# Reordering the parts of a time unit in a chunked recurrence on one Trainium2 core: output products to the unit's end, transposes moved together

## The chip, the core and the metric

One NeuronCore of a Trainium2 chip runs the whole program. The metric is device time in microseconds; lower is better. Engine names as in the profile: PE (TensorE) matmuls, PEld its weight loads, DVE (VectorE), ACT (ScalarE), POOL (GpSimd), SP (SyncE, which issues the DMAs here).

## What is computed

A linear recurrence over 768 tokens for 4 x 8 heads with a 40 x 40 state, then two feed-forward layers. Cut to what matters:

```python
for t in range(S):                                   # S = 768
    y[:, :, t] = np.einsum('bhd,bhde->bhe', rt, state)
    Sa = np.einsum('bhde,bhe->bhd', state, at)
    state_decay = state * wt[:, :, None, :] - np.einsum('bhd,bhe->bhde', Sa, bt)
    state = state_decay + np.einsum('bhd,bhe->bhde', vt, kt)
...
x = relu(x @ w_in); x = (x * sigmoid(conv3(x))) @ w_out          # layer 1
h = relu(x @ w_in2); out = (u * (w_spatial @ norm(v) + b)) @ w_out2   # layer 2
```

The change touches the recurrence alone.

## The kernel before

The tokens are cut into 6 groups of 128 (two chunks of 64 each) and the batch into 4, which gives 24 units kk = 0 .. 23 of 8 heads each (`units`, line 390). Two units of one token group with neighbouring batches make a pair, which shares its loads and its tiles. Four generators hold a unit's work, and each `yield` in them ends a part:

- `A` (lines 148 to 183), 5 parts, prepares a unit 9 units ahead (LA=9): 8 transposes of AR and their two scaled copies (tile bdA, L157, L159); then for each half of the heads four transposes of P and a copy to PT by ACT (L167, L168), two parts; then for each half four products of PT with bdA, masked by DVE into G (L174, L175), two parts. After the last one of a pair, four stores of G's triangles to DRAM are due 3 parts later (L181, TBL=3).
- `Bp` (231 to 297), 4 parts from token group 1 on, for the unit kk+1: pf and its copies (L272, L275, L278), px and its copies into bdN (L284, L287), then two parts of pw (L295) with their scaled copies WT by ACT (L296).
- `Cp` (317 to 343), 4 parts, carries the state: pu (L327) and its copies to Z by ACT (L329), pm (L338) and two DVE steps to the next VM (L340, L342), once per chunk.
- `Dp` (344 to 388), 6 parts, makes the output of the unit kk-1: z0, z1 (transposes pz and pv, L360, L366, and ACT's copies), S0, S1 (products pS, L373, masked by DVE into SS, L374), y0, y1 (16 pairs of small products each into one PSUM tile py, L381, L383); after y1 DVE multiplies py into lnA (L385), and for a pair's second unit a store of x is due 2 parts later (L387).

`run`'s main loop (line 478) is a hand-written order: the string ORDER has 19 letters, and part z takes the next part of the generator that the letter names. After each part `tick` issues what has come due, `pump` runs 1.25 steps on average of a background list (a triangular solve, `subst`, L206 and L208 on DVE, which is present in some units and absent in others), and the table SCHED, chosen by the parity of kk, starts the loads of the pair 5 pairs on. In even units these are il, araw, lnA, the product G (POOL), `dup`, P (l_P, L115) and `ar`; in odd units the one entry is "pm": `l_pm` (L145), the product of the whole P tile with the decays il, on DVE (PMV=1).

Since LA=9, A in an odd unit prepares the first unit of a pair, whose P has just been multiplied in that same unit; A in an even unit prepares the pair's second unit. A runs in the units 0 to 14 (unit 0 prepares two). Units 15 to 23 have no A; there the preparation of the next layer's weights (`later_layer`) fills DVE and ACT.

In this part of the program every engine runs in the order in which the code issues; all tiles named "ps" share 6 PSUM buffers, P has 6 buffers, ZV, bdR, SS and PT two, bdA, bdN and il one. Unit 9 is the stretch from 262.59 to 278.19 us of the trace, unit 11 begins at 293.89; both are odd, 9 with the background solve and 11 without it until late.

Of the kernel before, what the change touches and what calls it, by code (L numbers as in the profile page):

```python
# [11 lines left out]
def attention(tc, keep, ident, vr,bk,w,a, x, spare=None):  # L12
# [4 lines left out]
    with ExitStack() as ctx:  # L17
# [71 lines left out]
        def tick():  # L89
            now[0]+=1  # L90
            for d in [d for d in due if d[0]<=now[0]]:
                due.remove(d); d[1]()
# [300 lines left out]
        def pump(m):  # L393
            while m>0 and (bg or bg2):
                q=bg or bg2
                try: next(q[0])
                except StopIteration: q.pop(0); continue
                m-=1
# [10 lines left out]
        with tc.manual_schedule(engines={mybir.EngineType.SP,mybir.EngineType.DVE,mybir.EngineType.Activation}):  # L409
# [58 lines left out]
            with tc.manual_schedule():  # L468
# [9 lines left out]
                for kk in range(NK):  # L478
# [6 lines left out]
                    z=-1  # L485
                    for g in ORDER if kk<TAIL else ORDER2:
                        if g=='W':
# [7 lines left out]
                        tick(); acc+=RATE0 if kk<3 else RATE if kk<14 else RATE2; pump(int(acc)); acc-=int(acc)  # L495
                        for s,f in SCHED[(kk+LA+1)%2]+SCHEDC[kk%2]:
                            if s==z:
# [13 lines left out]
PUA=1  # L511
WM=2
ORDER2="DCCDDBCBACDADDABBAA"
ORDER="CDCBDDCBDDACABBDAAA"
LA=9
L4T=14
RATE=1.25
RATE2=1.25
RATE0=1.4
SCHED=[[[1, "il"], [11, "araw"], [12, "ln"], [14, "g"], [15, "dup"], [16, "P"], [17, "ar"]], [[5, "pm"]]]  # L520
SCHEDC=[[[6, "Z"]], [[10, "V"]]]
SUB=5
TBL=3
# [543 lines left out]
```

## Time and profile before

| | |
|---|---|
| timed runs, median (lowest to highest) | 960.11 us (960.07 to 965.37) |
| the profiled execution's own time | 955.54 us |
| its span, first to last instruction | 953.8 us |
| mean granted TensorE clock | 0.948 |
| busy in the span: PE / PEld / DVE / ACT / POOL | 91% / 83% / 69% / 56% / 21% |

The profiled execution is one run of its own, 4.6 us below the median of the timed ones. The units of the recurrence lie between 100 and 483 us; before them are loads and the first units' preparation, behind them the two layers. A busy share is an average over these stages.

### The profile page before, as it was taken

Reading aid. Unit: us, or ns where it says so; the run is one execution under the profiler, and the core shown is the slowest. Engines: PE = TensorE matmul, PEld = TensorE weight load, DVE = VectorE, ACT = ScalarE, POOL = GpSimd, SP = SyncE. Lnnn points to the kernel's source line nnn. Section 1 sums busy time; section 2 is a strip of 40 time slices with the busy share of each in tenths; the row PEclk is TensorE's granted clock in tenths of the full one; section 3 lists DMA queues with packets and bytes.
Section 4 is the critical chain, followed back from the end, with each engine's and each line's share of the span. In section 5 each row is a group of like instructions: output and inputs, shape, how many; then the busy total and the mean of one; then the engine's idle time right before and its main releaser. Section 6 shows DMA issues by size and latency. Waiting matters only on the chain. (4 is left out here: it accounts for less than half of the span.)

```text
span 953.8 us, 23470 instructions
## 1 busy us (share of the span) xinstructions
PE 863.3 (91%) x9575; PEld 793.1 (83%) x9575; DVE 661.8 (69%) x1503; ACT 535.7 (56%) x1166; POOL 204.9 (21%) x268
## 2 busy tenths in 40 slices
PE   0877699999999998989897799999999899998997
PEld 0566588999999998878786689998999889998997
DVE  6886785596794968976769976388725877368841
ACT  0444567778677776578655663366515654266521
POOL 2100110112111212123310002144223431234221
PEclk9975589999999998899989999999999999999999
DMA  8988594646557546235411320111001100011001
GB/s 215 211 187 225 121 212 101 153 91 152 110 124 178 95 99 156 65 103 131 125 63 58 107 80 19 42 48 36 23 25 42 56 1 26 21 53 32 1 1 45
DMA packets 149189, 86.70 MB, mean 91 GB/s; under 512 B 124176, under 2 KB 138256, under 8 KB 147152
## 3 DMA queue, kind: packets, MB, share of 16 engines
q1 hardware_dynamic: 148800, 84.78, 36.3%
q8 instruction: 77, 1.26, 0.6%
q14 instruction: 40, 0.33, 0.1%
q10 hardware_dynamic: 272, 0.33, 0.1%
HBM read 61.24 MB, written 23.86 MB: 89 GB/s over the span
## 5 line engine op out<-in xcount | busy, mean ns | idle before, releaser
L690 PE MATMUL psp<-spt,vv 128*128 128x384 f32 x576 | 105.6, 338 | 0.5 <-DVE vv L818 0.3
L690 PE MATMUL ph<-XT,G 128*128 128x386 f32 x512 | 101.9, 344 | 0.8 <-DVE XT L723 0.8
L690 PEld LDWEIGHTS psp<-spt,vv 128*128 128x128 f32 x576 | 100.2, 188 | 2.2 <-ACT vv L815 1.1
L690 PEld LDWEIGHTS ph<-XT,G 128*128 128x128 f32 x512 | 93.1, 192 | 1.3 <-DVE XT L723 1.0
L766 PE MATMUL acc<-gh,G 128*128 128x384 f32 x320 | 70.9, 347 | 17.1 <-ACT gh L750 9.3
L752 POOL TENSOR_TENSOR gl<-c,gh 128x384 fp32r<-128x384 f32 x48 | 66.3, 1381 | 90.0 <-ACT gh L750 78.1
L331 POOL COPY ZU<-ZU 64x320 f32<-64x320 f32 x48 | 25.7, 535 | 245.6 <-ACT ZU L329 245.6
L766 PEld LDWEIGHTS acc<-gh,G 128*128 128x128 f32 x320 | 55.6, 189 | 25.7 <-ACT gh L750 13.4
L835 DVE TENSOR_TENSOR psp<-psp,bb 128x384 f32<-128x384 f32 x32 | 18.1, 566 | 70.6 <-PE psp L690 70.5
L206 DVE TENSOR_TENSOR tmp<-L 128x30 f32<-128x30 f32 (+9 forms) x150 | 58.4, 389 | 8.6 <-DMA L<-tb 4.7
L748 DVE TENSOR_TENSOR c<-h,c 128x384 f32<-128x384 f32 x64 | 39.3, 614 | 33.2 <-ACT c L745 33.0
L750 ACT CAST gh<-c 128x384 fp32r<-128x384 f32 x64 | 32.9, 514 | 52.4 <-DVE c L748 51.0
L174 PE MATMUL p<-PT,bdA 80*128 80x128 f32 x384 | 57.3, 306 | 4.6 <-ACT PT L168 4.2
L174 PEld LDWEIGHTS p<-PT,bdA 80*128 80x128 f32 x384 | 52.6, 215 | 8.8 <-ACT PT L168 8.6
L373 PE MATMUL pS<-bdR,ZV 80*128 80x128 f32 x384 | 56.3, 291 | 2.8 <-ACT ZV L367 2.8
L839 ACT CAST zh<-u 128x384 fp32r<-128x384 f32 x28 | 14.4, 513 | 73.2 <-DVE u L836 73.2
L208 DVE TENSOR_TENSOR L<-L,tmp 128x30 f32<-128x30 f32 (+9 forms) x150 | 52.4, 349 | 3.8
L381 PE MATMUL py<-P,SS 128*64 128x40 f32 x768 | 52.2, 240 | 2.8 <-DVE SS L374 2.5
L295 PE MATMUL pw<-bdN,G 128*104 128x128 f32 x384 | 52.4, 295 | 1.0 <-issue 0.9
L373 PEld LDWEIGHTS pS<-bdR,ZV 80*128 80x128 f32 x384 | 48.5, 198 | 4.6 <-ACT ZV L367 3.3
L383 PE MATMUL py<-ZV,bdR 80*64 80x40 f32 x768 | 51.1, 237 | 0.0
L840 POOL TENSOR_TENSOR zl<-u,zh 128x384 fp32r<-128x384 f32 x28 | 28.6, 1020 | 101.0 <-ACT zh L839 91.5
(185 smaller groups left out, 2093.3 us busy)
## 6 DMA issues: line engine op xcount, KB each, us to landing
P<-in_bk_dram SPq DMA_DIRECT2D x12, 640.0 KB, 5.8
ZU<-in_vr_dram SPq DMA_DIRECT2D x12, 640.0 KB, 7.0
lq<-in_w_dram SPq DMA_DIRECT2D x12, 320.0 KB, 6.9
araw<-in_a_dram SPq DMA_DIRECT2D x12, 320.0 KB, 6.8
lam<-lq SPq DMA_DIRECT2D x12, 320.0 KB, 5.0
lnA<-lam SPq DMA_DIRECT2D x12, 320.0 KB, 7.7
ilam<-lq SPq DMA_DIRECT2D x12, 320.0 KB, 5.6
il<-ilam SPq DMA_DIRECT2D x24, 160.0 KB, 4.3
```

Of the source, the lines that this page charges most:

```text
L174: T.matmul(p3[:,j],lhsT=bdA[:,g*4+j].rearrange("p c t -> p (c t)"),rhs=PTs[g][:,j],start=True,stop=True)
L206: V.tensor_tensor(t,L[:,j+1:HB,j:j+1].to_broadcast([128,m,j]),L[:,j:j+1,0:j].to_broadcast([128,m,j]),ALU.mult)
L208: V.tensor_tensor(L[:,j+1:HB,0:j],L[:,j+1:HB,0:j],t,ALU.add)
L295: T.matmul(p[:104,j],lhsT=G[:,h0+g*4+j,C:],rhs=N[:,g*4+j],start=True,stop=True)
L373: T.matmul(p[:,j].rearrange("p c t -> p (c t)"),lhsT=ZV[:,j,0:2*C],rhs=bdR[:,j].rearrange("p c t -> p (c t)"),start=True,stop=True)
L381: T.matmul(py[c*C:(c+1)*C,h],lhsT=SS[:,j,c],rhs=P[:,h0+h,c],start=True,stop=False)
L383: T.matmul(py[c*C:(c+1)*C,h],lhsT=bdR[:,j,c],rhs=ZV[:,j,2*C:],start=False,stop=True)
L690: L.tc.nc.tensor.matmul(out,lhsT=l,rhs=r,start=start and i==0,stop=stop and i==len(prs)-1)
L748: V.tensor_tensor(c,h[:,1:TH+1],c,ALU.mult)
L750: AC.copy(gh,c)
L752: def low(v): v.tensor_tensor(gl,c,gh.bitcast(F32),ALU.subtract)
L766: nc.tensor.matmul(acc[m],lhsT=l,rhs=r,start=f==0 and z<5 and z in (0,1,3),stop=f==NF-1 and z>=5)
```

## The change

Three settings change; no operation is added or taken away. With the 19 parts numbered 0 to 18:

- D's last two parts, y0 and y1, go from the places 9 and 15 to 17 and 18, the end of the unit. A goes from 10, 12, 16, 17, 18 to 9, 11, 12, 15, 16, so that its two P transposes stand together ahead of the two pw parts (13, 14 as before). C's last part (pm of the second chunk) goes from 11 to 10.
- P's load (even units) goes from 16 to 18, since the buffer that it takes is released by y1 of the same unit.
- P's product with the decays (odd units) goes from 5 to 8.

```diff
-ORDER="CDCBDDCBDDACABBDAAA"
+ORDER="CDCBDDCBDACAABBAADD"
...
-SCHED=[[[1, "il"], [11, "araw"], [12, "ln"], [14, "g"], [15, "dup"], [16, "P"], [17, "ar"]], [[5, "pm"]]]
+SCHED=[[[1, "il"], [11, "araw"], [12, "ln"], [14, "g"], [15, "dup"], [18, "P"], [17, "ar"]], [[8, "pm"]]]
```

On PE, in an A-carrying unit (unit 10), from px to the products of PT (rows of the first py part are left out; pS, p_.. with AR, pm and p_.. with P are the parts S1, bdA, pm and the transposes of P):

```order
-L157 MATMUL p_4026<-ident,AR 80x64 x8
-L338 MATMUL pm<-ZU,P 40x40 x8
-L167 MATMUL p_4053<-ident,P 80x128 x4
+L284 MATMUL px<-F,D_3541 32x32 x16
+L373 MATMUL pS<-bdR,ZV 128x128 x4
+L157 MATMUL p_4009<-ident,AR 80x64 x8
+L338 MATMUL pm<-ZU,P 40x40 x8
+L167 MATMUL p_4034<-ident,P 80x128 x4
+L167 MATMUL p_4043<-ident,P 80x128 x4
 L295 MATMUL pw<-bdN,G 104x128 x8
```

The transposes of AR now follow S1 directly, and the second group of P transposes stands ahead of pw instead of behind y1; the sixteen py rows that stood around these now stand behind the last PT product, directly ahead of the next unit's pu.

On DVE, in unit 9 (SS are the masked pS parts, L206 and L208 the background solve, P the product with the decays, m and VM the two steps behind pm):

```order
 L374 TENSOR_TENSOR SS<-pS,mS 128x512
 L206 TENSOR_TENSOR tmp<-L 128x228
-L145 TENSOR_TENSOR P<-P,il 128x1280
 L208 TENSOR_TENSOR L<-L,tmp 128x12x19
...
 L374 TENSOR_TENSOR SS<-pS,mS 128x512
 L206 TENSOR_TENSOR tmp<-L 128x210
+L145 TENSOR_TENSOR P<-P,il 128x1280
 L208 TENSOR_TENSOR L<-L,tmp 128x10x21
+L340 TENSOR_TENSOR m<-pm,VM 40x320
+L342 TENSOR_TENSOR VM<-m,lamC 40x8x40
```

The product of P stood between the first and the second masked pS and now stands behind the second.

On SP, at the end of an even unit (D is a load for the solve's results, tb the stores of G's triangles, x the store of the output):

```order
-L229 DMA D_4071<-dd_129 32x16x32 x2
-L387 DMA x<-lnA 128x2x320
-L115 DMA P<-in_bk_dram 128x1280
+L229 DMA D_4061<-dd_129 32x16x32 x2
 L181 DMA tb_124<-G 32x16x32 x4
+L115 DMA P<-in_bk_dram 128x1280
+L387 DMA x<-lnA 128x2x320
```

P's load was issued ahead of the four triangle stores and is now issued behind them, and x's store goes from ahead of P's load to behind it.

## Rows read from the trace of the kernel before

**Rows 1.** Busy time by stage; columns: window, length, then PE, PEld, DVE, ACT, POOL, clock, DMA

```profile
190.00:340.00 150.00, 149.17 (x2634) 136.86 (x2634) 116.51 (x270) 111.04 (x238) 26.09 (x42) 1.00 0.58 123
356.00:483.00 127.00, 115.50 (x2109) 105.81 (x2106) 93.92 (x192) 84.65 (x212) 36.37 (x63) 0.92 0.45 118
```

**Rows 2.** PE in order of time, unit 9; columns: start, length, work

```profile
270.00 0.32 PE L381 MATMUL py<-P,SS 128*64 128x40 f32 x4
...
271.06 0.64 PE L157 MATMUL p<-ident,AR 64*80 64x64 f32 x8
271.63 0.81 PE L338 MATMUL pm<-ZU,P 128*40 128x40 f32 x16
272.37 0.64 PE L167 MATMUL p<-ident,P 128*80 128x128 f32 x4
272.84 1.91 PE L295 MATMUL pw<-bdN,G 128*104 128x128 f32 x16
274.68 0.32 PE L381 MATMUL py<-P,SS 128*64 128x40 f32 x4
...
275.74 0.64 PE L167 MATMUL p<-ident,P 128*80 128x128 f32 x4
```

**Rows 3.** DVE in order of time, unit 9

```profile
269.04 0.69 DVE L374 TENSOR_TENSOR SS<-pS,mS 128x512 f32<-128x512 f32 x1
...
269.95 1.49 DVE L145 TENSOR_TENSOR P<-P,il 128x1280 f32<-128x1280 f32 x1
271.35 0.39 DVE L208 TENSOR_TENSOR L<-L,tmp 128x228 f32<-128x228 f32 x1
...
272.50 0.68 DVE L374 TENSOR_TENSOR SS<-pS,mS 128x512 f32<-128x512 f32 x1
```

**Rows 4.** DVE in order of time, unit 11, with the idle time before and its releaser

```profile
301.02 0.69 DVE L374 TENSOR_TENSOR SS<-pS,mS 128x512 f32<-128x512 f32 x1 [0.22 <-PE pS L373]
```

**Rows 5.** PE in order of time, the last product of unit 8 and unit 9's start

```profile
260.39 2.27 PE L174 MATMUL p<-PT,bdA 80*128 80x128 f32 x16
262.59 0.67 PE L327 MATMUL pu<-VM,WT 104*64 104x40 f32 x16
```

**Rows 6.** PE in order of time, unit 0 and units 15 and 16

```profile
126.39 2.05 PE L174 MATMUL p<-PT,bdA 80*128 80x128 f32 x16 [0.88 <-ACT PT L168]
...
364.03 0.32 PE L381 MATMUL py<-P,SS 128*64 128x40 f32 x4 [1.00 <-DVE SS L374]
...
364.99 0.78 PE L338 MATMUL pm<-ZU,P 128*40 128x40 f32 x16
...
375.36 0.67 PE L327 MATMUL pu<-VM,WT 104*64 104x40 f32 x16 [1.18 <-DVE VM L342]
...
378.67 0.44 PE L381 MATMUL py<-P,SS 128*64 128x40 f32 x4
...
380.40 1.27 PE L338 MATMUL pm<-ZU,P 128*40 128x40 f32 x16
```

**Rows 7.** All waits, 100 to 484 us: engine, line, releaser, total, times, longest

```profile
PEld pm L338 <- ACT ZU L329: 5.0, 16, 1.3
```

**Rows 8.** DMA issues on SP at unit 10's end, and P's load issue to landing

```profile
292.58 0.44 SPq L387 DMA_DIRECT2D x<-lnA  x1
293.11 0.42 SPq L115 DMA_DIRECT2D P<-in_bk_dram  x1
294.72 2.07 SPq L181 DMA_DIRECT2D tb<-G  x4
...
DMA to landing us min/median/max: 4.2/5.8/8.8
```

**Rows 9.** Busy time in three short stretches, columns as in rows 1

```profile
372.90:376.40 3.50, 2.32 (x57) 2.11 (x56) 3.25 (x10) 2.04 (x7) 0.18 (x1) 1.00 0.68 134
...
376.40:383.20 6.80, 6.80 (x79) 6.43 (x73) 5.76 (x15) 0.98 (x3) 0.45 (x1) 0.50 0.40 61
...
403.70:407.10 3.40, 2.15 (x36) 1.92 (x30) 3.13 (x10) 2.43 (x7) 0.42 (x2) 1.00 0.11 23
```

## The prediction, made before the changed kernel was run

> **What bounds the kernel now.** I read the busy time by stage first. From 190 to 340 us, the heart of the recurrence, PE is busy 149.2 of 150.0 us with the clock at its full level [rows 1]: there nothing can be won by filling gaps, only by making the parts themselves shorter, and every wait that the change puts before PE is paid in full. From 356 to 483 us PE has 11.5 us of idle time and a mean clock of 0.92 [rows 1]; there fillers can pay. Behind 483 us the change does nothing. Next I read PE in order of time through one odd unit [rows 2] and DVE beside it [rows 3], since an odd unit is where P's product with the decays moves, then DVE in an odd unit without the background solve [rows 4].
>
> **Parts that come closer together on PE.** A y part takes 0.96 us where the next part has small products too (364.03 to 364.99, [rows 6]), but 1.06 us where transposes follow it (270.00 to 271.06, and 274.68 to 275.74, [rows 2]): a change of the kind of product costs about 0.10 us. In a unit with A the order was S1, y0, bdA, pm, P transposes, pw, y1, P transposes, G products, pu; it becomes S1, bdA, pm, P transposes, pw, G products, y0, y1, pu. The joints y0-bdA, pw-y1 and y1-P transposes go, three of 0.10 us, in 14 units (1 to 14): -4.2 us. No row shows the joint S1-bdA or P transposes-P transposes apart; bounds for the whole term are 0 and 6.
>
> **G products that waited for PT.** In unit 8 the two G parts take 2.20 us (260.39 to 262.59, [rows 5]), while sixteen instructions of the same 128-column shape, pw, take 1.84 us (272.84 to 274.68, [rows 2]). The second G part waits for ACT's copy of the second PT, which was issued just ahead. With pw between the transposes and the G parts that copy is long done: 0.36 us in the six even units 2 to 12, -2.2 us. Unit 0 has one such wait on its own, 0.88 us [rows 6]: -0.9 us.
>
> **The units without A.** y0 in unit 15 waits 1.00 us for the masked SS; put behind pm and pw it would not. pu in unit 16 waits 1.18 us for VM [rows 6], which DVE reaches late; DVE's multiply behind y1 now comes after more of its background work, so some of this goes as well. But DVE is the late engine there, busy 93.9 of 127 us in bursts, and a PE that arrives sooner waits again for it: between 0 and -2.2 us, I take -1.5 us. The price on the other side: pm of the second chunk loses the cover of y0 (0.96 to 1.06 us) against ACT's copy of Z. Such waits are there already, 16 of 5.0 us in all [rows 7]; each could grow by up to 1 us, or not at all. I take +1.0 us.
>
> **P's product, the term that decides.** The first P transposes of an odd unit cannot start before the product is done (1.49 us on DVE, [rows 3]). Before, it stood behind the first SS, at 269.95 us in unit 9, and its reader came at 272.37 us: a spare 0.9 us after the product's end. Now it stands behind the second SS. With PE going on at 270.00 us, where y0 stood, bdA takes 0.57 us and pm 0.74 us [rows 2], so PE wants P at 271.31 us. DVE, if as late as now, starts the second SS at 272.50 - 1.40 = 271.10 us (the product no longer ahead of it), then 0.69 for the mask, 0.39 for one solve step and 1.49 for the product [rows 3]: 273.67 us, so PE waits 2.4 us. If DVE were not late, SS would start with PE's 270.00 and a tenth, and the wait would be 1.4 us. I take 1.9 us for the three odd units in the middle of a solve (5, 9, 13). Without the solve (3, 7, 11) DVE starts the second SS as soon as S1 ends, at 301.02 us [rows 4], and needs 0.69 + 1.49 = 2.18 us, while PE needs 0.57 + 0.74 = 1.31 us: 0.9 us each. Unit 1 is between 0 and 2.4 us; I take 1.0. Sum: 5.7 + 2.7 + 1.0 = +9.4 us. Behind the waiting transposes on PE stand the second group, pw, G, both y and the next unit's pu, all of which shift; behind them on DVE stand m and VM, which nobody wants before the next token group; ACT's PT and WT copies wait with PE.
>
> **P's load and the queues.** It waits for y1 of the even unit to free its buffer, so it moves from 293.11 us, 0.8 us ahead of the unit's end (unit 11 begins at 293.89), to just behind it, and on SP now stands behind four triangle stores that take 2.07 us to issue [rows 8]; their G is ready two y parts ahead of the unit's end, so I put the load's issue at 0.9 to 1.3 us into the odd unit. With the median of 5.8 us to landing [rows 8] it is there at about 7 us; the product's place on DVE is 7.8 us (301.71 - 293.89) without the solve, later with it. So the load costs nothing, with a cover of under 1 us. What is pushed back on SP is x's store, which nobody reads before the layers. ZV, bdR and SS are overwritten one unit on, behind y1 on PE's own queue: no cost. py now holds its PSUM buffer for two parts instead of seven; no row shows a wait for one, so I count nothing.
>
> **The clock.** After a stretch in which PE was busy 2.32 of 3.50 us, the clock went to its lower level, 1.2 GHz, for 6.8 us [rows 9]; in there a y part takes 1.73 us (378.67 to 380.40) instead of 0.96 [rows 6]. So 6.8 us at that level lose 6.8 x (1 - 0.96/1.73) = 3.0 us where PE sets the pace. After 2.15 busy of 3.40 us it stayed at the full level, 2.4 GHz [rows 9]. A wait of 1.9 us is longer than all the idle time of either stretch (1.18 and 1.25 us), so I expect falls behind it in two of the three units, +6.0 us, with 0 and 7 falls as bounds. The Trainium skill, "TensorE: Matmul & The Clock Gate", Part 4 (PE-mode transpose), says that transposes do not count as PE being busy in the way that products do. By it every odd unit would fall, since its wait would stand between transposes on both sides, which is rival 2; no run here shows the rule by itself yet, and the full clock from 190 to 340 us, transposes and all [rows 1], does not speak for it.
>
> **Sum.** -4.2 - 2.2 - 0.9 - 1.5 + 1.0 + 9.4 + 6.0 = +7.6 us. On the profiled execution, 955.5 us, that is 963.1 us; the timed runs lie 4.6 us above it in the median, and on their 960.1 us it is 967.7 us.
>
> **Rivals.** (1) The waits come, but no fall of the clock: +1.6 us, 961.7 us. For it: idle stretches without a fall exist [rows 9]. (2) Each of the seven odd units falls, since wait, bdA and P transposes stand in one row: 1.6 + 7 x 3.0 = +22.6 us, 982.7 us. Against it: the light units' 0.9 us of idle is less than any stretch in rows 9 shows. (3) On the other side: DVE, which no longer has y's multiply between its solve steps at that place, runs ahead, and the product is done when PE wants it, so the 9.4 us fall away with their falls of the clock: -7.8 us, 952.3 us. It decides if the product ends within 1.31 us of S1; the mask and the product alone take 2.18 us, which speaks against it, unless PE is itself held up elsewhere ahead of P. (4) P's load lands late, after 8.8 us, the longest seen [rows 8], from an issue at 1.2 us: product's end at 11.5 us into the unit against 8.7 wanted (271.31 - 262.59), 2.8 us in seven units, 19.6 instead of 9.4, and seven falls: +32.8 us, 992.9 us. Against it: the middle one of the loads landed after 5.8 us [rows 8].
>
> **How the numbers follow.** The forecast, with its own range of 964 to 972 us, has 0.40; rival 1 0.24, rival 2 0.18, rival 3 0.10, rival 4 0.08. A measurement of this kernel tells about 1%, 9.6 us, from no change. Slower by more (over 969.7): rivals 2 and 4 and a third of the forecast, 0.40. Faster by more (under 950.5): half of rival 3, 0.05. Within: 0.55. The range 954 to 984 us holds all but rivals 3 and 4.
>
> **What would show it.** Right: PE idle ahead of the P transposes (L167), released by DVE's product (L145), some 2 us in units 5, 9, 13 and 1 us in 3, 7, 11; G parts of 1.9 us in even units; y0 and y1 as one block of 2.0 us; lower clock in the recurrence behind the longest waits. Wrong: L167 released by nothing, or by the DMA of P; G parts of even units still at 2.2 us; or the clock at its full level through 160 to 340 us.

## The result, and the profile after

The changed kernel takes 968.96 us in the median of 13 timed runs (963.23 to 972.67), beside 960.18 us for the kernel before in 13 runs (957.76 to 968.15): the ratio is 1.0089, with a 95% interval of 1.0068 to 1.011. A ratio here and below compares fast runs alone, so it is not quite the quotient of the medians, which hold the slow runs too (one each in experiments 2, 3, 7 and 11). The forecast was 967.7 us. So it is slower by 0.9%, in the case to which the prediction gave the most, but not quite by the terms of its sum.

The profiled execution after took 968.96 us (span 967.2 us, mean clock 0.938), the one before 955.54 us, which lies 4.6 us below the median of its kernel. So the two traces differ by 13.4 us where the medians differ by 8.8; terms are compared below on the traces.

Busy time by stage (columns as in [rows 1]): the heart of the recurrence after, then the units 15 to 22, which have no A, before and after. These units begin 16 us later in the changed kernel, so each trace has its own window for them:

```profile
190.00:340.00 150.00, 140.40 (x2500) 131.34 (x2498) 107.31 (x249) 106.94 (x229) 25.47 (x43) 0.97 0.53 113
...
355.61:461.54 105.93, 98.61 (x1874) 90.55 (x1874) 80.87 (x171) 72.84 (x177) 27.80 (x45) 0.94 0.44 111
...
371.96:475.06 103.10, 96.68 (x1880) 89.31 (x1876) 80.63 (x171) 73.17 (x177) 27.85 (x46) 0.93 0.44 115
```

In the heart of the recurrence PE was busy 149.17 of 150 us and is now busy 140.40, at a clock of 0.97 instead of 1.00. The units without A became 2.8 us shorter: PE's busy time there fell by 1.9 us and its idle time by 0.9. What PE waits for between 100 and 484 us (total, times, longest) names one new item of weight, the first below; beside it only two single new waits of PE are over 1 us, 2.7 us for AR in unit 0 and 1.4 us for lnA in unit 18:

```profile
PE p L167 <- DVE P L145: 16.2, 8, 3.3
...
PE pu L327 <- DVE VM L342: 6.3, 7, 2.1
...
PEld pm L338 <- ACT ZU L329: 4.2, 13, 0.9
```

PE in order of time, the end of unit 8 and unit 9 (269.51 to 290.68 us), to be held against [rows 2, 5]:

```profile
265.74 1.95 PE L174 MATMUL p<-PT,bdA 80*128 80x128 f32 x16
267.62 0.32 PE L381 MATMUL py<-P,SS 128*64 128x40 f32 x4
...
269.51 0.64 PE L327 MATMUL pu<-VM,WT 104*64 104x40 f32 x16
...
275.67 1.16 PE L373 MATMUL pS<-bdR,ZV 80*128 80x128 f32 x8
276.76 0.64 PE L157 MATMUL p<-ident,AR 64*80 64x64 f32 x8
277.33 0.81 PE L338 MATMUL pm<-ZU,P 128*40 128x40 f32 x16
281.41 1.90 PE L167 MATMUL p<-ident,P 128*80 128x128 f32 x8 [3.27 <-DVE P L145]
283.10 3.62 PE L295 MATMUL pw<-bdN,G 128*104 128x128 f32 x16
```

The G parts of unit 8 take 267.62 - 265.74 = 1.88 us (2.20 before, [rows 5]); both y parts together take 269.51 - 267.62 = 1.89 us (two of 1.06 before, [rows 2]); both P transposes stand together. Then, in the odd unit, PE stands still for 3.27 us ahead of them. After it pw takes 3.4 us instead of 1.84, at the lower clock. The same 3.27 us stand in units 5 and 13, and 0.97, 0.91 and 0.97 us in units 3, 7 and 11. DVE in order of time, the same unit, against [rows 3]:

```profile
271.50 0.48 DVE L385 TENSOR_TENSOR lnA<-py,lnA 128x320 f32<-128x320 f32 x1
...
276.70 0.69 DVE L374 TENSOR_TENSOR SS<-pS,mS 128x512 f32<-128x512 f32 x1
...
278.89 0.69 DVE L374 TENSOR_TENSOR SS<-pS,mS 128x512 f32<-128x512 f32 x1
279.49 0.37 DVE L206 TENSOR_TENSOR tmp<-L 128x210 f32<-128x210 f32 x1
279.77 1.49 DVE L145 TENSOR_TENSOR P<-P,il 128x1280 f32<-128x1280 f32 x1
```

DVE has no idle time in this stretch. It multiplies the y that was made in unit 8 (271.50) only inside unit 9, reaches the first SS 7.19 us into the unit (6.45 before) and the second 9.38 us in, though PE had ended S1 by 276.8. One unit earlier, S1 of unit 8 on PE and its mask on DVE, in the kernel before and in the changed one:

```profile
253.09 1.16 PE L373 MATMUL pS<-bdR,ZV 80*128 80x128 f32 x8
...
254.29 0.69 DVE L374 TENSOR_TENSOR SS<-pS,mS 128x512 f32<-128x512 f32 x1
...
260.69 1.16 PE L373 MATMUL pS<-bdR,ZV 80*128 80x128 f32 x8
...
261.89 0.69 DVE L374 TENSOR_TENSOR SS<-pS,mS 128x512 f32<-128x512 f32 x1
```

DVE is on time there in both, right behind S1. From this mask to the first SS of unit 9 it takes 269.04 - 254.29 = 14.75 us before and 276.70 - 261.89 = 14.81 us after, with y's multiply inside the stretch both times. PE, from the end of this S1 to unit 9, takes 262.59 - 254.25 = 8.34 us before and 269.51 - 261.85 = 7.66 us after. Without the solve, in unit 11 (it begins at 305.92), DVE waits for S1 instead, as in [rows 4], and goes straight on to the product:

```profile
313.03 0.69 DVE L374 TENSOR_TENSOR SS<-pS,mS 128x512 f32<-128x512 f32 x1 [1.61 <-PE pS L373]
313.63 1.48 DVE L145 TENSOR_TENSOR P<-P,il 128x1280 f32<-128x1280 f32 x1
```

The issues on SP at unit 8's end, and the landing of P's loads, against [rows 8]:

```profile
270.15 1.97 SPq L181 DMA_DIRECT2D tb<-G  x4
272.21 0.45 SPq L115 DMA_DIRECT2D P<-in_bk_dram  x1
272.76 0.39 SPq L387 DMA_DIRECT2D x<-lnA  x1
...
DMA to landing us min/median/max: 4.8/5.2/8.8
```

The load is issued 2.70 us into the unit; with the median landing of 5.2 us it is there at 277.4, 2.4 us ahead of the product. The lower clock, against [rows 9], in the window around unit 9's pw:

```profile
280.50:287.30 6.80, 5.89 (x28) 5.76 (x29) 4.45 (x11) 2.30 (x4) 0.00 (x0) 0.50 0.72 139
```

In units 5 and 13 the clock fell as well, for 3.4 us each (215.7 and 348.8 us); in units 3, 7 and 11 it did not.

By units (from pu to pu), the two traces add up as follows; the third column is the prediction's sum, sorted by the same units.

| units | measured after - before, us | predicted, us |
|---|---|---|
| 0 to 2 | 72.66 - 69.88 = +2.8 | -0.9 |
| 5, 9, 13 (solve, product) | 61.78 - 46.59 = +15.2 | +10.8 |
| 3, 7, 11 (product, no solve) | 47.22 - 45.64 = +1.6 | +1.8 |
| even, 4 to 14 | 90.60 - 93.38 = -2.8 | -3.6 |
| 15 to 22 (no A) | 103.10 - 105.93 = -2.8 | -0.5 |
| all | 375.36 - 361.42 = +13.9 | +7.6 |

The units 5, 9 and 13, called heavy below (3, 7 and 11 are the light ones), carry the loss, and they are what the experiments look at. Unit 0 says little: it is between 26.5 and 32.0 us long in the traces of this study, at the lower clock for much of it.

### The profile page after: what moved, and what is told of

Same layout as the page of the kernel before. It is cut to its first block, busy times and chain, and to the rows that moved or that the text cites. A ratio compares the mean times of both kernels' runs of the same rounds, so it can differ in the third digit from the quotient of the medians.

```text
span 967.2 us, 23480 instructions
## 1 busy us (share of the span) xinstructions
PE 864.1 (89%) x9575; PEld 798.3 (83%) x9575; DVE 661.5 (68%) x1503; ACT 537.2 (56%) x1166; POOL 203.0 (21%) x268
## 5 line engine op out<-in xcount | busy, mean ns | idle before, releaser
L690 PE MATMUL psp<-spt,vv 128*128 128x384 f32 x576 | 105.6, 338 | 0.5 <-DVE vv L818 0.3
L331 POOL COPY ZU<-ZU 64x320 f32<-64x320 f32 x48 | 23.6, 492 | 262.3 <-ACT ZU L329 262.2
L175 DVE TENSOR_TENSOR G<-p,mT 128x512 f32<-128x512 f32 x48 | 32.8, 689 | 42.4 <-PE p L174 39.3
L208 DVE TENSOR_TENSOR L<-L,tmp 128x30 f32<-128x30 f32 (+9 forms) x150 | 56.8, 379 | 3.9
L295 PE MATMUL pw<-bdN,G 128*104 128x128 f32 x384 | 57.4, 313 | 1.2 <-issue 1.1
L206 DVE TENSOR_TENSOR tmp<-L 128x30 f32<-128x30 f32 (+9 forms) x150 | 53.1, 354 | 5.3 <-DMA L<-tb 1.5
L295 PEld LDWEIGHTS pw<-bdN,G 128*104 128x104 f32 x384 | 54.1, 205 | 2.2 <-issue 1.5
L329 ACT COPY ZU<-pu 64x160 f32<-64x160 f32 x96 | 27.5, 287 | 43.6 <-PE pu L327 42.0
```

Source lines behind the costliest of these rows:

```text
L175: V.tensor_tensor(G[:,hs,0:2*C],p3,mT.rearrange("p a t -> p (a t)").unsqueeze(1).to_broadcast([128,4,2*C]),ALU.mult)
L206: V.tensor_tensor(t,L[:,j+1:HB,j:j+1].to_broadcast([128,m,j]),L[:,j:j+1,0:j].to_broadcast([128,m,j]),ALU.mult)
L208: V.tensor_tensor(L[:,j+1:HB,0:j],L[:,j+1:HB,0:j],t,ALU.add)
L295: T.matmul(p[:104,j],lhsT=G[:,h0+g*4+j,C:],rhs=N[:,g*4+j],start=True,stop=True)
L329: for q in range(2): AC.copy(Z[0:64,h0+q:h0+H:2,c],pu[q*64:q*64+64,q:H:2])
L690: L.tc.nc.tensor.matmul(out,lhsT=l,rhs=r,start=start and i==0,stop=stop and i==len(prs)-1)
```

## The experiments

All were timed in three rounds (the last in five) beside the kernel before, whose median was 957.9 to 959.3 us in those sets. "Place" is a part's number in ORDER or in SCHED. The theory: PE arrives earlier at the P transposes, and the product, behind the second SS in DVE's queue, is late by what DVE has still to do. The rivals: P's load lands late; the transposes standing together cost the time or the clock; the falls of the clock are most of it.

**1. The product back at place 5, the new order kept.**

```diff
-... [[8, "pm"]]]
+... [[5, "pm"]]]
```

> The changed kernel with P's product with the decays back at part 5 of odd units; the new order and the later load stay. Theory 1 (the product stands too far back in DVE's queue, behind the second mask and the background solve): the waits of the P transposes (L167) for the product, 16.2 us in the changed kernel, fall to 3 to 6 us (from 3.27 to about 1.2 us in units 5, 9, 13, from 0.97 to about 0 in 3, 7, 11), the clock falls in these units go too, and the time is 957 to 962 us. Theory 2 (P's load, now issued 1.7 to 2.7 us into the odd unit and landing 4.8 to 6.2 us later, sets when the product can start): DVE shows a wait of the product for the DMA of P, the waits of PE stay above 10 us in all, and the time is 965 to 970 us.

Measured: 961.0 us, ratio 1.0009 (0.9977 to 1.0041). Waits of PE for the product, and of the product for its load:

```profile
PE p L167 <- DVE P L145: 6.7, 5, 2.1
DVE P L145 <- DMA P<-in_bk_dram: 5.3, 4, 1.8
```

16.2 us of waits become 6.7, a little over the 3 to 6 us expected, and nearly the whole 0.9% goes with them. Product and second SS have only changed places on DVE, so it is the place in the queue that costs. Of what is left, 1.73 us stand in unit 0. In units 5 and 9 PE waits 1.11 us each though no load holds the product: DVE is late there without it. In units 11 and 13 (0.60 and 2.13 us) the product itself waits for P's load, which the change has also put later. No run puts the product at place 8 in the old order, so what that place costs by itself isn't known.

**2. The triangle stores put off, so that P's load no longer stands behind them.** The product stays at place 8.

```diff
-TBL=3
+TBL=6
```

> The changed kernel with the triangle stores due 6 instead of 3 parts later, so that P's load is again issued ahead of them; product still at part 8. Theory 1 (place in DVE's queue): P lands some 2 us sooner and nothing changes, 967 to 971 us, L167 waits 15 to 17 us. Theory 2 (landing): the waits shrink by up to 2 us in each of seven units, 955 to 963 us.

Measured: 967.64 us, ratio 1.0065 (1.0032 to 1.0098).

```profile
PE p L167 <- DVE P L145: 14.6, 8, 3.3
```

P's load is issued 0.10 us into each odd unit from 3 on, and the waits stay (units 3, 7, 11 still 0.97, 0.92 and 0.97 us, unit 13 3.27). With the product at 8, the landing is not what it waits for: rival 4 falls. Units 5 and 9 wait less, 2.16 and 2.75 us, but not for the load's sake: in this trace PE takes 10.44 and 8.28 us from the end of S1 in units 4 and 8 to the next unit (7.66 in the changed kernel), so DVE had more time to come up. Where PE was slower ahead of the heavy unit, the wait was shorter.

**3. Both: the product at 5 and the stores put off.**

> Both: product at part 5 and triangle stores due 6 parts later. Theory 1: as with the product at 5 alone or up to 2 us less, since the load was there anyway. Theory 2: here, and only here, the waits vanish: 953 to 960 us, at least 5 us below the run with the product at 5 alone. If the gains that were forecast for the order (shorter G parts, fewer joints, 7 us in all in the units with A) are real and no wait is left, both give about 953 us against 960 before.

Measured: 958.98 us, ratio 0.9992 (0.9958 to 1.0025). Of the waits for the product only unit 0's is left, but PE now loses time elsewhere:

```profile
PE pu L327 <- DVE VM L342: 9.6, 6, 2.4
...
PE p L167 <- DVE P L145: 1.7, 1, 1.7
```

The next bound is DVE's VM, and units 4 and 12 are 19.67 and 21.08 us long, with a stop of PE of 1.6 to 1.8 us in each that no semaphore explains (below), and falls of the clock behind it.

**4. The transposes together, the outputs left where they were** (on the kernel before; P's load at 17, the product at 5).

```diff
-ORDER="CDCBDDCBDDACABBDAAA"
+ORDER="CDCBDDCBDDACAABBDAA"
```

> The kernel before with one part moved: the second group of P transposes joins the first ahead of pw; y0 and y1 stay at 9 and (now) 16, the product at 5, P's load at 17. Theory (the G parts of even units waited for ACT's copy of the second PT, 0.36 us each, and each joint of unlike products costs 0.1 us): 2 to 4 us less than before, 956 to 958 us, G parts 1.84 to 1.95 us. Rival (the transposes ahead of pw bring no gain because pw and the copies of WT come later, or PE waits for something else): 960 us or more.

Measured: 956.76 us, ratio 0.997 (0.9937 to 1.0003). Heart of the recurrence, columns as in [rows 1]:

```profile
190.00:340.00 150.00, 148.40 (x2623) 136.99 (x2621) 117.12 (x271) 110.72 (x239) 26.83 (x44) 1.00 0.57 122
```

Units 4, 8 and 12 take 15.18 or 15.19 us (15.44 before), there is no wait for the product, and the clock stays at its full level with eight transposes in a row. This half of the change costs nothing and perhaps brings 0.3%.

**5. PE kept busy through the wait:** 14 dummy products, 28 matmuls, ahead of the first P transposes in units 5, 9 and 13 of the changed kernel. They are extra work and feed nothing.

```diff
+                        if z==11 and kk in (5,9,13): warm(ident,14)
```

> The changed kernel with 14 matmuls of the identity, whose result nobody reads, ahead of the P transposes in units 5, 9 and 13 alone, about 3.05 us of PE work in place of the wait of 3.27 us there. Theory (the clock falls behind these waits are a cost of their own): the wait shrinks to under 0.5 us, the clock stays at its full level in these three units (13.6 us at the lower level in the changed kernel, of which about 6 us is lost), and the time is 961 to 965 us. Rival (DVE sets the pace there, a slower PE costs nothing): 967 to 971 us.

Measured: 963.64 us, ratio 1.0045 (1.0012 to 1.0078).

```profile
276.83 3.39 PE L408 MATMUL warm<-ident 128*128 128x128 f32 x28
280.17 1.04 PE L167 MATMUL p<-ident,P 128*80 128x128 f32 x8
281.05 1.91 PE L295 MATMUL pw<-bdN,G 128*104 128x128 f32 x16
```

The transposes start no sooner, but the clock stays up and pw takes its 1.75 us again. Units 5, 9 and 13 take 18.63, 18.27 and 18.63 us, 55.5 in all instead of 61.8: 6.3 us on the traces are the clock's share of the loss, 5.3 us by the medians of the two kernels, 4.4 us if each is held against the kernel before of its own set. The rest is the wait itself.

**6. DVE's work in front of the product made less:** the half of the copies of DT into bdN that DVE does (L278, two in a unit, 0.57 us; the recorded texts call them px's source copies, but it is pw that reads bdN) goes to POOL, in the changed kernel.

```diff
-                (G_.tensor_copy if q%2 else V.tensor_copy)(N[qs,:,...
+                G_.tensor_copy(N[qs,:,...
```

> The changed kernel with the two copies of DT into bdN that DVE makes in each unit (0.6 us, L278) given to POOL, which makes the other two. Theory (DVE is behind in the units with the solve, and its lag is part of the 3.27 us wait): the wait in units 5, 9, 13 falls by 0.6 to 1.8 us, that in 3, 7, 11 stays at 0.97 us, 962 to 966 us. Rival (only the product's place counts): waits as before, 967 to 971 us.

Measured: 966.4 us (four timed runs), ratio 1.0115 (1.0058 to 1.0173), so no gain in time that can be told. The wait itself answers clearly:

```profile
275.43 1.90 PE L167 MATMUL p<-ident,P 128*80 128x128 f32 x8 [2.66 <-DVE P L145]
```

3.27 us become 2.65, 2.66 and 2.66 in the heavy units, 0.6 us less, about what was taken off DVE in one unit, while units 3, 7 and 11, where DVE has time, keep 0.97, 0.91 and 0.97. The heavy wait is DVE's backlog; the light one is the chain S1, mask, product.

**7. Product at 5, stores put off, copies to POOL** (3 and 6 together).

> The new order with the product at part 5 and the stores later, and the DT copies on POOL. There units 8 and 12 wait about 1 us for VM on DVE and the clock falls behind these waits. Theory (with the product out of the way DVE's load in the solve units is what takes the order's gain back): VM waits and most falls in units 4 to 13 go, even units at 14.7 us throughout, 951 to 955 us. Rival: 957 to 961 us, as without it.

Measured: 951.85 us (948.19 to 964.37), ratio 0.9936 (0.9903 to 0.9968): 0.6% faster than the kernel before and, by the two ratios, 1.5% faster than the changed one. Its profiled execution, with a span of 959.5 us, lies high in that spread, and it shows only half of what was expected: the product is waited for in unit 0 alone and the odd units 3 to 13 take 14.7 to 15.1 us, but the even units 4 to 14 take 15.6 to 21.4 us, not 14.7 throughout. Four of them hold a stop of PE without a semaphore, the longest in unit 12:

```profile
312.58 0.62 PE L272 MATMUL pf<-DT,G 32*32 32x32 f32 x26
315.18 0.28 PE L272 MATMUL pf<-DT,G 32*32 32x32 f32 x6 [1.98 <-issue]
```

Whether the faster executions lack these stops, no trace shows.

**8. The transposes together, copies to POOL** (4 and 6 together).

> The kernel before with the second P transposes ahead of pw (956.8 us) and the DT copies on POOL. Theory: PE is busy without a gap in units 3 to 14 there, so DVE's relief brings little: 953 to 957 us, the gain coming from units 15 to 18 alone. Rival (DVE's lag costs PE in these units too, unseen): 950 to 952 us.

Measured: 956.02 us, ratio 0.9971 (0.9943 to 1.0): the same as 4 alone. With the outputs at their old places DVE's lateness hardly reaches PE (1.0 us of waits for the masked SS between units 3 and 14 in 4, none here), and relieving it brings no gain that can be told.

**9. The other half alone: the outputs at the end, the transposes apart** (product at 5, P's load at 18).

```diff
-ORDER="CDCBDDCBDDACABBDAAA"
+ORDER="CDCBDDCBDACABBAAADD"
```

> The kernel before with only y0 and y1 moved to places 17 and 18 (and P's load to 18, which must follow y1); A at 9, 11, 14, 15, 16, so that the second P transposes stay behind pw as before, and P's product at place 5 as before. It is the fourth corner beside the kernel before, the transposes alone and both together with the product at 5. Theory (outputs at the end uncover P's product even at place 5, because the load's landing and DVE's lateness are against it in the heavy units; the transposes only bring their gain): PE waits for the product 4 to 8 us in all, the G parts of even units wait for PT again (2.2 us a part pair instead of 1.9), time 961 to 965 us, that is above both together (961.0). Rival (the outputs at the end are free once the product stands at 5): 955 to 959.5 us, and waits for the product under 2.5 us in all.

Measured: 963.27 us, ratio 1.0049 (1.0023 to 1.0075).

```profile
PE p L167 <- DVE P L145: 7.4, 5, 2.4
```

Even at place 5 the product is waited for, once nothing of y stands ahead of the transposes. Of this 1.7 us stand in unit 0. With 1 and 4 this makes four corners, all with the product at 5: neither half 1.000, the transposes 0.997, the outputs 1.0049, both 1.0009. So with the product at 5 what is lost is lost by the outputs; the larger part of the 0.9% came with place 8 (experiment 1). In the units without A the outputs' move wins: in all traces of this study units 15 to 22 take 102.4 to 105.6 us with the outputs at the end and 105.9 to 109.8 us with them at their old places.

**10. Control: the kernel before with the copies on POOL.**

> The kernel before with the half of px's source copies that DVE does (line 278) given to POOL, nothing else. It is the control for the two runs that did the same beside a changed order. Theory (DVE is late only where PE waits for it, and the kernel before hardly waits for it in the recurrence): within 0.5% of the kernel before, 956 to 961 us, units 3 to 13 at 15.2 to 15.6 us as before. Rival (the copies off DVE are by themselves what brings the gain of 0.6% of the best run): 950 to 955 us.

Measured: 958.63 us, ratio 0.9997 (0.9971 to 1.0022): nothing. So 7's gain is not that of the copies by themselves.

**11. As 7, but the stores as before** (TBL=3).

> The changed kernel with P's product back at place 5 and DVE's half of px's source copies given to POOL; the triangle stores stay due 3 parts after A, as before. It is the best run so far (951.85 us) with the stores not put off, so it tells whether that run needed the later stores. Theory (in units 5, 9 and 13 the product at place 5 waits for P's landing, and P's load stands behind the four stores; only putting the stores off lets it land in time): PE waits for the product 4 to 7 us in all from 100 to 484 us, as with the product at 5 alone (6.7), and the time is 956 to 961 us. Rival (the copies were what held DVE back, and the stores put off only pile up other loads, behind which PE's stops of 1 to 2 us without a semaphore stand): waits for the product under 3 us, no such stop above 1 us, time 948 to 953 us.

Measured: 957.68 us, ratio 0.9984 (0.9949 to 1.0019).

```profile
DVE P L145 <- DMA P<-in_bk_dram: 7.6, 5, 2.1
PE p L167 <- DVE P L145: 7.3, 7, 2.1
```

The load's landing holds the product again, in units 1, 3, 9, 11 and 13. Run 7 takes all three together: the product early on DVE, its load early on SP, and DVE with less in front. With one of the last two left out (3 and 11) the ratio is 0.999 and 0.998; their intervals overlap run 7's a little, so how much each brings isn't settled.

## Why the prediction was right, and where its sum was not

**Parts closer together: right, and rather small.** Units 8 and 12 went from 15.43 and 15.44 to 14.73 and 14.72 us: 0.7 us, where joints and PT were put at 0.30 + 0.36. Units 3, 7 and 11 went from 15.21 to 15.74 us with a wait of 0.9 to 1.0 in them, so the rest became 0.4 shorter (0.3 forecast). Units 6, 10 and 14 kept less of it, 0.3 to 0.5 us; they follow the heavy ones. Unit 4 kept 0.07 us, with a wait of 0.34 us ahead of its second pu.

**Units without A: right in sign, too small.** -2.8 us instead of -1.5 + 1.0. The price on the other side did not come: PE's loads for pm wait 4.2 us in 13 instead of 5.0 in 16 [rows 7]. Waits of y for the masked SS, 1.9 us in 3 before, are gone from units 15 to 22 as forecast, but those for VM grew there from 3.0 to 4.0 us (3 each): DVE is still the late engine. The larger part, 1.9 us, is less busy time of PE, which the sum left out for these units.

**The product without the solve: right.** 0.97, 0.91 and 0.97 us stand against the 0.9 worked out from one mask and one product.

**The product with the solve: the step that was mis-sized.** The prediction took 1.9 us between bounds of 1.4 and 2.4; it was 3.27 in each of the three units, outside both. The step was "DVE, if as late as now" as the upper bound. Set from the unit's start: PE wants P at 8.63 us (281.41 - 3.27 - 269.51), near the forecast 8.72, but the product ends at 11.75 (279.77 + 1.49 - 269.51) instead of 11.08 us, and PE goes on 0.15 us behind that, which the sum had at nothing. DVE's own work did not shrink when PE's units did: from unit 8's second SS to unit 9's first it takes 14.8 us in both traces, while PE's way from that S1 to unit 9 became 0.68 us shorter (7.66 against 8.34), so DVE stood 0.74 us further back at the first SS (7.19 against 6.45 us). A faster PE made the waited-for engine later. Experiment 6 confirms it, since less for DVE in front shortens exactly this wait, and experiment 2 from the other side, where a slower PE ahead of it shortens it.

**Units 0 and 1: partly missed.** Unit 1's wait was 1.80 us (1.0 forecast). Unit 0, which also multiplies P, waits 1.73 us; no term stood for that.

**The clock: right in sum, not in count.** Two falls of 6.8 us, 6.0 us in all, were forecast. There were three, of 3.4, 6.8 and 3.4 us, 13.6 us in all, and experiment 5 puts their price at 4.4 to 6.3 us. The light units' 0.9 us of idle time brought no fall. So rival 2 did not happen, and the rule named beside it, of the Trainium skill ("TensorE: Matmul & The Clock Gate", Part 4 (PE-mode transpose)), by which transposes don't count as PE being busy as products do, is not what decides here: the clock stayed at 1.00 through eight transposes in a row in experiment 4, and between units 3 and 14 of the changed kernel it fell only behind the idle 3.27 us. The prediction put these waits between transposes on both sides; in fact the products of pm stand directly ahead of them (277.33 above). Elsewhere less idle time was followed by a fall too: 1.18 us in the kernel before [rows 9].

**P's load: right in result, wrong in its issue.** It was issued 2.7 us into units 5, 9 and 13 and 1.7 us into unit 11, not 0.9 to 1.3 (that holds for unit 7 alone, 0.92), because the stores wait for G's masks on the same late DVE. It still came over 2 us ahead of its use in unit 9. The cover was there only because the product was later too: at place 5 it is gone (experiments 1 and 11).

**Rival 3 fell.** That DVE no longer has y's multiply between its solve steps "at that place" gained it nothing: the multiply left unit 8 only to stand in front of unit 9's first mask, and the product ended 4.4 us after S1 (276.83 to 281.26), not within 1.31 us.

On the traces the sum was 6.3 us short (7.6 against 13.9), most of it the heavy waits (9.8 against 5.7 us); that the median came within 1.3 us of the forecast owes something to the low execution that served as the trace of before.

## What to carry to other kernels

Work that is moved away from in front of a waiting reader was its cover: before you move it, work out from both engines' queues, from the start of the unit, when the reader wants the data and when its producer's turn comes. Where the producing engine has no idle time, a gain on the reader's side is added to its lateness (0.68 us gained, 0.74 us later here), so "as late as now" is a lower bound of the wait, not an upper one. And a move that needs three others (the product's place, its load's place behind other issues, less on DVE) can lose by itself and win with them: 0.9% slower alone, 0.6% faster in run 7.

## What the runs showed of the hardware

**PE stops where no semaphore is.** From unit 3 on, the traces of experiments 1, 3, 7 and 9, all with the outputs at the end, show stops of 0.6 to 2.0 us put down to "issue", most of them within a run of like matmuls (1.98 us at 313 us above). The other traces have none of that length there; in units 1 and 2 most kernels have one, the one before too (0.80 us). In experiment 7 the DMAs were busy just ahead of the longest:

```profile
305.00:312.50 7.50, 7.50 (x136) 7.18 (x134) 3.81 (x13) 4.28 (x11) 0.81 (x2) 1.00 1.13 215
312.60:315.20 2.60, 0.62 (x30) 0.51 (x29) 2.08 (x5) 0.66 (x2) 1.35 (x3) 1.00 0.92 164
```

The queue of instructions moved two packets in the window from 311 to 317 us. The stops come back at the same place in the code: after 26 of pf's 32 matmuls in unit 12 in experiments 1, 3 and 7, after 17 of them in unit 6 in experiments 3 and 7. That PE's instructions came late behind the loads would fit this, but no run tested it, and the kernel before speaks against its being enough: with a DMA share of 1.01 from 305 to 312.5 us and two packets of instructions from 311 to 317 us it has no stop there. The cause stays open.

**A solve step of DVE beside POOL's product took four times as long.** All engines of the changed kernel in order of time:

```profile
266.05 1.75 POOL L121 TENSOR_TENSOR G<-araw,lnA 128x640 f32<-128x640 f32 x1 [4.68 <-DVE L L208]
266.42 1.63 DVE L208 TENSOR_TENSOR L<-L,tmp 128x228 f32<-128x228 f32 x1
```

The same step takes 0.39 us elsewhere. This happens once in each of units 4, 8 and 12, so 1.2 us ahead of each heavy unit, in the kernel before too (1.63 to 1.64 us). The Trainium skill ("GPSIMD Engine Reference", section 1, Specifications) says that POOL shares its SBUF interfaces with VectorE and contends with its instructions that have two SBUF inputs; the row agrees, with 1.63 against 0.39 us. In units 6 and 10, without the solve, what DVE does beside the same product has one input in PSUM, and takes its usual time (the mask of G 0.69 us in unit 6). The slow step is a part of DVE's backlog that neither kernel removes.
